# Threshold attention and a squared-ReLU layer: rounding instructions, thresholds and a bank order moved

## Chip, cores and metric

One core of a Trainium2 chip runs the whole program. The metric is the device time of one execution in microseconds (us), smaller is better. A core has five engines that run their own queues side by side: TensorE (PE, matrix products; PEld is its weight load), VectorE (DVE), ScalarE (ACT), GpSimd (POOL) and SyncE (SP, which issues most DMAs). SBUF is the on-chip memory, PSUM the eight banks that TensorE writes.

## What is computed

Batch 8, 8 heads, 576 positions, head width 64. For every head

```
scores = q @ k.T / 8
keep   = scores >= rowmax(scores) - tau
attn   = exp(where(keep, scores, -1e9) - rowmax);  attn /= rowsum + 1e-9
x      = attn @ v                       # heads side by side: 4608 x 512
out    = relu(x @ w_in)**2 @ w_out      # 512 -> 2048 -> 512
```

All data are float32; the two weight matrices come in as 64-bit words whose two halves the kernel combines ("rounding").

## The kernel before

**Attention** is worked in visits and steps. A visit is a pair of heads of one batch; a step is one block of 128 query rows of that visit. The first four visits have two steps each (steps 0 to 7), the next four have three (steps 8 to 19), the later ones four or five. In a step TensorE makes the scores in PSUM (`scores`, L280 or L273), VectorE takes two row maxima (`maxima`, L317), ScalarE takes the exponentials into `w`, VectorE masks them with the threshold and sums them (`threshold`, L354, then L356 for the sum and L357 for the reciprocal), and GpSimd divides (`divide`, L362 and L364). Two steps later TensorE transposes `w` (`turn`, L408), ScalarE copies that out (L409), and the values are mixed (`mix`, L524).

The threshold is `maximum - 8 tau`. In the early steps (`early_exponents`, steps 0 to 10) VectorE adds it for both columns (L329), with the constant `ntau8` that GpSimd scaled at the start (L1036); then ScalarE makes a bias (L332) and an exponential (L333) for each of the two halves of the step. In later steps (`exponents`) ScalarE makes bias (L339), threshold (L340) and exponentials (L342).

**Weights** come in 32 pieces into a ring of three areas and are rounded in stages (`round_weights`): stage 0 is two ScalarE instructions (L149, L150), stage 1 a shift and stage 2 a mask on VectorE (L152, L154), stage 3 a product on GpSimd (L156), and `end_rounding` adds and places the piece on GpSimd (L158) and loads the next. An early step does stage 0 for its own piece and the other stages for the piece of the step before, after `threshold` and `divide`. From step 11 on a step rounds one piece, but four steps (12, 15, 18 and 22) round two.

**The layer** is worked in chunks of 256 tokens: `mlp_in` (L571), a square (L581, L582), then for chunk 0 `mlp_out` (L753, copied out by L759) and for later chunks products of halves (L788). A planner, `fill`, puts as many of these pieces into each step as an estimated rate asks for; it knows costs written in the source, not measured times, so the order of work is fixed when the program is built.

**Banks.** Chunk 0 takes banks 6 and 7 of PSUM in turn (`take`), later work takes the bank that was used longest ago (`next_bank`, from the list `oldest`, which `last_used` reorders).

What an early step ends with, and the middle of a later one:

```
threshold(n, i)
divide(n, i)
while rounding:
    p = rounding.popleft()
    for stage in (1, 2, 3):
        round_weights(p, stage)
    end_rounding(p)
```

Each engine takes its instructions in the order in which the source issues them; waits on other engines are semaphores.

Of the kernel before, what the change touches and what calls it, by code (L numbers as in the profile page):

```python
# [9 lines left out]
FP32 = mybir.dt.float32  # L10
U32 = mybir.dt.uint32
AF = mybir.ActivationFunctionType
ALU = mybir.AluOpType
# [6 lines left out]
def kernel(  # L20
# [10 lines left out]
    nc = tc.nc  # L31
# [3 lines left out]
    P = 128  # L35
# [11 lines left out]
    SCALE = 0.125  # L47
# [4 lines left out]
    const = ctx.enter_context(tc.tile_pool(name="const", bufs=1))  # L52
# [2 lines left out]

    ident = const.tile([P, P], FP32, name="ident")
    seen = const.tile([P, 1], FP32, name="seen")
    ntau8 = const.tile([P, 2], FP32, name="ntau8")

    w_in_sb = const.tile([P, NMC, d_ff], FP32, name="w_in_sb")  # L60

# [19 lines left out]
    at = RAW * 2 * WP  # L81
# [24 lines left out]
    bank = [big[:, x * 512:(x + 1) * 512] for x in range(8)]  # L106
# [14 lines left out]
    def weight_piece(i):  # L121

        if i < n_in:
            f, c = BLK[i // NMC], i % NMC
            cols = slice(f * WP, (f + 1) * WP)
            return moe_w_in[c * P:(c + 1) * P, cols], w_in_sb[:, c, cols].rearrange("p (h d) -> p h d", h=2)
        i -= n_in
        to = wo[:, Q00:Q01 + 1:Q01 - Q00, i, :] if i < HF else wo[:, Q10:Q11 + 1, i - HF, :]
        return moe_w_out[i * P:(i + 1) * P, :], to

    def weight_area(i):
        at = (i % RAW) * 2 * WP
        return spare[:, at:at + 2 * WP]
# [4 lines left out]
    def round_weights(i, stage):  # L138

        words = weight_area(i).bitcast(U32).rearrange("p (n w) -> p n w", w=2)
        lo, hi = words[:, :, 0], words[:, :, 1]
        t, e, d = (turned[:, (i % 3 * 3 + x) * WP:(i % 3 * 3 + x + 1) * WP] for x in range(3))
        tu, eu = t.bitcast(U32), e.bitcast(U32)
        if stage == 0:
            nc.scalar.activation(out=e, in_=hi.bitcast(FP32), func=AF.Prelu, scale=2.0 ** -112, alpha=-2.0 ** 32)  # L149
            nc.scalar.activation(out=d, in_=lo, func=AF.Copy, scale=2.0 ** -52)  # L150
        elif stage == 1:
            nc.vector.tensor_scalar(out=tu, in0=eu, scalar1=3, scalar2=None, op0=ALU.logical_shift_left)  # L152
        elif stage == 2:
            nc.vector.tensor_scalar(out=eu, in0=tu, scalar1=0xFF800000, scalar2=None, op0=ALU.bitwise_and)  # L154
        elif stage == 3:
            nc.gpsimd.tensor_tensor(out=d, in0=d, in1=e, op=ALU.mult)  # L156
        else:
            nc.gpsimd.tensor_tensor(out=weight_piece(i)[1], in0=t.rearrange("p (h d) -> p h d", h=2),  # L158
                                    in1=d.rearrange("p (h d) -> p h d", h=2), op=ALU.add)
# [166 lines left out]
    def early_exponents(vis, i):  # L326

        w, sc, st = weights[vis, i]
        nc.vector.tensor_tensor(out=st[:, 1, 0:len(sc)], in0=st[:, 0, 0:len(sc)], in1=ntau8[:, 0:len(sc)], op=ALU.add)  # L329
        for u in range(len(sc)):  # L330
            bias = st[:, 2, u:u + 1]
            nc.scalar.activation(out=bias, in_=st[:, 0, u:u + 1], func=AF.Copy, scale=-SCALE)  # L332
            nc.scalar.activation(out=w[:, u, :].rearrange("p (h k) -> p h k", h=2), in_=sc[u],  # L333
                                 func=AF.Exp, bias=bias, scale=SCALE)

    def exponents(vis, i):
        w, sc, st = weights[vis, i]
        mx, thr, bias = (st[:, j, 0:len(sc)] for j in range(3))
        nc.scalar.activation(out=bias, in_=mx, func=AF.Copy, scale=-SCALE)  # L339
        nc.scalar.activation(out=thr, in_=mx, func=AF.Identity, bias=ntau8[:, 0:1])  # L340
        for u in range(len(sc)):
            nc.scalar.activation(out=w[:, u, :].rearrange("p (h k) -> p h k", h=2), in_=sc[u],  # L342
                                 func=AF.Exp, bias=bias[:, u:u + 1], scale=SCALE)

    def threshold(vis, i):

        w, sc, st = weights[vis, i]
        n = len(sc)  # L350
        thr, sm, den, rcp = (st[:, j, 0:n] for j in (1, 3, 5, 6))
        for u in range(n):
            wu = w[:, u, :].rearrange("p (h k) -> p h k", h=2)
            nc.vector.scalar_tensor_tensor(out=wu, in0=sc[u], scalar=thr[:, u:u + 1], in1=wu,  # L354
                                           op0=ALU.is_ge, op1=ALU.mult, accum_out=sm[:, u:u + 1])
        nc.vector.tensor_reduce(out=den, in_=st[:, 3:5, 0:n].rearrange("p j u -> p u j"), axis=AX.X, op=ALU.max)  # L356
        nc.vector.reciprocal(rcp, den)  # L357

# [8 lines left out]
    used = {"tx": 0, "mm": 0, "bank": 7}  # L367
# [2 lines left out]

    def take(what, among):
        used[what] += 1
        return bank[among[used[what] % len(among)]]

    def next_bank():

# [5 lines left out]
    def last_used(x):  # L382
        oldest.remove(x)
        oldest.append(x)
# [464 lines left out]
    def by_dma(n):  # L849

        return n >= 3 * HP - 1
# [113 lines left out]
    for s, (n, i) in enumerate(steps):  # L965
        if s < HP * FIRST:
            x = int(n > 0 and i == 1)
        else:
            x = 0 if s == early_to - 1 else 2 if (n, i) in ((HP + 1, FIRST + 1), (2 * HP - 2, FIRST + 1), (2 * HP - 1, FIRST + 1), (2 * HP, FIRST)) else 1
# [49 lines left out]

    load_qk(0)  # L1020
    make_identity(nc, ident)
    nc.gpsimd.dma_start(out=ntau8[:, 0:1], in_=tau.to_broadcast([P, 1]))
    nc.gpsimd.memset(qmid, 0.0)
    for t in vs:
        for u in range(2):
# [6 lines left out]
    load_v(0)  # L1032
    for i in range(RAW):
        load_weights(i)
    for x in (1, 0):
        nc.gpsimd.tensor_scalar(out=ntau8[:, x:x + 1], in0=ntau8[:, 0:1], scalar1=-1.0 / SCALE, scalar2=None, op0=ALU.mult)  # L1036
    keep_busy(20, 7)
    done = 0
    rounded_by = [0]
# [89 lines left out]
    def early_step(s):  # L1129


        n, i = steps[s]
        first, last = i == visits[n][1][0], i == visits[n][1][-1]
        now = list(range(sum(pieces[:s]), sum(pieces[:s + 1])))
        if first and n and n + 2 < 2 * HP:
            load_qk(n + 2)
        if s == 0:
            scores(0)()
            early_exponents(n, i)
            keep_busy(18, 7)  # L1140
            held_back.append(scores(1))
            prep_part(k, 1)
        elif s == 1:
            prep_part(q, 1)
            held_back.pop()()
            early_exponents(n, i)
            scores(2)()
            early_exponents(*steps[2])
        elif s > 2:
            scores(s)()  # L1150
            early_exponents(n, i)
        copies = [turn(*steps[s - 2], part) for part in range(3)] if s > 1 else []
        if s == 2:
            keep_busy(12, 4)
        if s > 1 and (first or n >= HP and i == FIRST + 1) and not (first and n >= HP):
            prep_part(k, n + 1)
        if s > 1 and last:
            prep_part(q, n + 1)
        for fn in copies:
            fn()  # L1160
        if s in mixes:
            mix(*mixes[s])
            for j in chunk_at.get(s, ()):
                add_chunk(j)
        if first:
            split_left(n)
        for p in now:
            round_weights(p, 0)
        threshold(n, i)
        divide(n, i)  # L1170
        while rounding:
            p = rounding.popleft()
            for stage in (1, 2, 3):
                round_weights(p, stage)
            end_rounding(p)
        rounding.extend(now)
        assert s < early_to - 1 or not now
        if first and n:
            load_v(n)

    rounding = deque()
    for s in range(END + 1):
# [13 lines left out]
        now = []  # L1196
        if on:
            n, i = steps[s]
            at = visits[n][1].index(i)
            last = at == len(visits[n][1]) - 1  # L1200
            now = list(range(done, done + pieces[s]))
# [18 lines left out]
        if on:  # L1220
            exponents(n, i)
            if s and by_dma(steps[s - 1][0]):
                turn_last(s)
            for p in now[1:]:
                round_weights(p, 0)
            if at == 1:
                split_left(n)
            if lay:
                prep(n + 1)
            elif now:  # L1230
                for p in now:
                    round_weights(p, 1)
        if s in mixes and not old:
            mix(*mixes[s])
            for j in chunk_at.get(s, ()):
# [15 lines left out]
        if on:  # L1251
            threshold(n, i)
            for fn in prep_at[s] + load_at[s]:
                fn()
            if lay and now:
                round_weights(now[0], 1)
            if now:
                round_weights(now[0], 2)
                round_weights(now[0], 3)
            for p in now[1:]:  # L1260
                assert not lay
                round_weights(p, 2)
                round_weights(p, 3)
            if not at_once:
                divide(n, i)
# [60 lines left out]
```

## Time and profile before

| what | value |
|---|---|
| median of 3 runs | 1328.32 us (1327.66 to 1328.34) |
| the profiled execution: its time, its span | 1329.19 us, 1327.4 us |
| TensorE busy | 1292.5 us, 97% of the span |
| VectorE busy | 936.9 us, 71% |
| GpSimd busy | 786.3 us, 59% |
| ScalarE busy | 582.4 us, 44% |
| L329, threshold adds | 11, 4.1 us |
| L152, L154, VectorE's part of the rounding | 32 each, 24.1 and 21.6 us |
| L156, L158, GpSimd's part | 32 each, 40.9 and 42.5 us |

A row of the profile's timeline gives the start in us, the duration in us, the engine, the line of the source, the operation, output and inputs with their shapes, and in brackets the idle time before it and what ended it. A row of the waits gives who waited for whom, the total, how often, and the longest. Busy times by stretch give, for a piece of the span, the busy us of each engine. A busy TensorE is not TensorE at its peak.

### The profile page before, as it was taken

Reading aid. Unit: us, or ns where it says so; the run is one execution under the profiler, and the core shown is the slowest. Engines: PE = TensorE matmul, PEld = TensorE weight load, DVE = VectorE, ACT = ScalarE, POOL = GpSimd, SP = SyncE. Lnnn points to the kernel's source line nnn. Section 1 sums busy time; section 2 is a strip of 40 time slices with the busy share of each in tenths; the row PEclk is TensorE's granted clock in tenths of the full one; section 3 lists DMA queues with packets and bytes.
Section 4 is the critical chain, followed back from the end, with each engine's and each line's share of the span. In section 5 each row is a group of like instructions: output and inputs, shape, how many; then the busy total and the mean of one; then the engine's idle time right before and its main releaser. Section 6 shows DMA issues by size and latency. Waiting matters only on the chain.

```text
span 1327.4 us, 24734 instructions
## 1 busy us (share of the span) xinstructions
PE 1292.5 (97%) x8862; PEld 1070.4 (81%) x8862; DVE 936.9 (71%) x2037; ACT 582.4 (44%) x1342; POOL 786.3 (59%) x917
## 2 busy tenths in 40 slices
PE   7899999999999999999999999999999999999998
PEld 5666556888887879697878888888887988889997
DVE  6978876887787878778776777868686877622131
ACT  4777774335352626253534353434343434331321
POOL 3789974874846564565665655646574737454351
PEclk9999999999999999999999999999999999999999
DMA  6764531757687869676766867767686766520000
GB/s 128 154 160 121 152 85 26 166 134 178 166 188 168 196 152 207 146 195 157 151 165 159 181 152 180 174 126 180 146 194 135 189 161 153 160 53 9 9 17 17
DMA packets 320907, 185.48 MB, mean 140 GB/s; under 512 B 282224, under 2 KB 282256, under 8 KB 314384
## 3 DMA queue, kind: packets, MB, share of 16 engines
q1 hardware_dynamic: 309120, 115.78, 46.1%
q0 software_dynamic: 10000, 67.92, 12.8%
q8 instruction: 70, 1.15, 0.4%
q14 instruction: 53, 0.43, 0.1%
q10 hardware_dynamic: 1664, 0.21, 0.1%
HBM read 108.04 MB, written 68.42 MB: 133 GB/s over the span
## 4 chain that ended last, share of the span: by engine, by line
PE 83%; DVE 6%; DMA 4%; ACT 2%; POOL 2%; issue 2%; SPq 1%; DVEq 0%; ACTq 0%; POOLq 0%
PE big L682 29%; PE big L788 28%; PE big L524 10%; PE big L296 8%; PE big L571 3%; PE big L280 2%; DVE st L317 2%; DMA wT<-aside 1%; PE big L753 1%; DMA aside<-turned 1%; DVE w L354 1%; PE big L408 1%; SPq L185 1%; ACT w L342 1%; POOL w_in_sb L158 0%
## 5 line engine op out<-in xcount | busy, mean ns | idle before, releaser
L354 DVE SCALAR_TENSOR_TENSOR w<-big,st,w 128x576 f32<-128x576 f32 x269 | 207.1, 805 | 88.1 <-ACT w L342 87.6
L317 DVE TENSOR_REDUCE st<-big 128x1 f32<-128x576 f32 x288 | 204.3, 748 | 88.8 <-PE big L296 60.7
L364 POOL TENSOR_SCALAR w<-w,st 128x576 f32<-128x576 f32 x269 | 244.9, 919 | 27.8 <-DVE st L357 22.3
L788 PE MATMUL big<-wo,gsum 128*128 128x256 f32 x1088 | 243.8, 382 | 0.0
L788 PEld LDWEIGHTS big<-wo,gsum 128*128 128x128 f32 x1088 | 204.4, 190 | 37.0 <-issue 7.6
L682 PE MATMUL big<-xT,w_in_sb 128*128 128x128 f32 x1536 | 187.4, 277 | 1.3 <-DVE g L694 1.2
L682 PEld LDWEIGHTS big<-xT,w_in_sb 128*128 128x128 f32 x1536 | 178.5, 192 | 10.5 <-issue 7.7
L788 PE MATMUL big<-wo,g 128*128 128x256 f32 x816 | 185.3, 382 | 0.1
L342 ACT ACTIVATE w<-big,st 128x576 f32<-128x576 f32 x255 | 174.2, 734 | 0.2 <-POOL t L659 0.2
L788 PEld LDWEIGHTS big<-wo,g 128*128 128x128 f32 x816 | 151.6, 190 | 26.1 <-issue 6.5
L524 PE MATMUL big<-wT,vs 128*64 128x256 f32 (+5 forms) x1420 | 159.6, 389 | 5.8 <-DMA wT<-aside 3.7
L524 PEld LDWEIGHTS big<-wT,vs 128*64 128x64 f32 (+1 forms) x1420 | 85.6, 136 | 71.7 <-issue 20.7
L362 POOL TENSOR_SCALAR st<-st 128x2 f32<-128x2 f32 (+1 forms) x148 | 35.6, 241 | 181.2 <-DVE w L354 169.8
L339 ACT ACTIVATE st<-st 128x2 f32<-128x2 f32 (+1 forms) x137 | 27.9, 204 | 250.1 <-DVE st L317 248.8
L430 POOL DMA_DIRECT2D aside<-turned x50 | 29.9, 597 | 177.9 <-DVE turned L459 171.8
L694 DVE TENSOR_TENSOR g<-big,g 128x512 f32<-128x512 f32 x96 | 64.7, 677 | 83.4 <-PE big L682 77.8
L296 PE MATMUL big<-kT,qT 64*128 64x256 f32 (+3 forms) x768 | 106.9, 416 | 0.0
L296 PEld LDWEIGHTS big<-kT,qT 64*128 64x128 f32 x768 | 84.5, 186 | 14.5 <-issue 5.0
L690 ACT ACTIVATE g<-g 128x512 f32<-128x512 f32 x96 | 60.3, 628 | 63.7 <-DVE g L694 63.6
L561 POOL TENSOR_TENSOR gsum<-g 128x512 f32<-128x512 f32 x34 | 46.1, 1356 | 69.8 <-ACT g L691 60.2
L691 ACT ACTIVATE g<-g 128x512 f32<-128x512 f32 x128 | 80.7, 630 | 4.1
L453 DVE STREAM_TRANSPOSE turned<-w 128x512 f32<-128x512 f32 x100 | 70.3, 703 | 0.3 <-issue 0.3
(118 smaller groups left out, 2063.4 us busy)
## 6 DMA issues: line engine op xcount, KB each, us to landing
aside<-turned POOLq DMA_DIRECT2D x50, 1152.0 KB, 4.8
wT<-aside SPq DMA_DIRECT2D x200, 288.0 KB, 5.4
vs<-in_v_dram SPq DMA_DIRECT2D x72, 128.0 KB, 5.9
wo<-in_moe_w_in_dram SPq DMA_DIRECT2D x16, 512.0 KB, 4.4
wo<-in_moe_w_out_dram SPq DMA_DIRECT2D x16, 512.0 KB, 3.6
out_dram<-osb POOLq DMA_DIRECT2D x32, 256.0 KB, 4.1
kl<-in_k_dram SPq DMA_DIRECT2D x113, 72.0 KB, 3.4
ql<-in_q_dram SPq DMA_DIRECT2D x112, 72.0 KB, 5.8
```

The lines of the kernel that those rows point to most:

```text
L296: nc.tensor.matmul(big[to, at + x0:at + x1], lhsT, keys[u * D:(u + 1) * D, x0:x1], start=True, stop=True)
L317: nc.vector.tensor_reduce(out=mx[:, u:u + 1], in_=sc[u], axis=AX.XY, op=ALU.max)
L342: nc.scalar.activation(out=w[:, u, :].rearrange("p (h k) -> p h k", h=2), in_=sc[u], func=AF.Exp, bias=bias[:, u:u + 1], scale=SCALE)
L354: nc.vector.scalar_tensor_tensor(out=wu, in0=sc[u], scalar=thr[:, u:u + 1], in1=wu, op0=ALU.is_ge, op1=ALU.mult, accum_out=sm[:, u:u + 1])
L364: nc.gpsimd.tensor_scalar(out=w[:, u, :], in0=w[:, u, :], scalar1=z[:, u:u + 1], scalar2=rcp[:, u:u + 1], op0=ALU.add, op1=ALU.mult)
L453: move(wb[:, 0:h, :, :], whole_[:, 0, :, :, :])
L524: nc.tensor.matmul(ps[u * D:(u + 1) * D, :], vs[n % 2][rows, u * (NBLK + 1) + c, :], wT[rows, at // REST:(at + ps.shape[1]) // REST, NBLK ...
L682: nc.tensor.matmul(to[:, f, :], factor(j, p, q, c)[:, f * P:(f + 1) * P], part[:, c, :], start=(p in "125" and f == 0 and c == 0), stop=(p ...
L690: nc.scalar.activation(out=to, in_=to if src is None else src, func=AF.Relu)
L691: nc.scalar.activation(out=to, in_=to, func=AF.Square)
L694: nc.vector.tensor_tensor(out=x, in0=to, in1=x, op=ALU.add)
L788: nc.tensor.matmul(to, left[:, f, :], wo[:, slot, f, :], start=(f == 0), stop=(f == HF - 1))
```

## The change

Four edits.

- VectorE's threshold add of the early steps becomes an identity with a bias on ScalarE, issued after the first exponential. `ntau8` has one column, scaled once.
- In early steps stages 1 and 2 of the waiting piece are issued after the masks and before the sum and the reciprocal (`between`). Stage 3 and the end stay behind the divide.
- In steps with two pieces stage 1 of the second piece is issued behind the masks, after stage 3 of the first piece, where it was ahead of the masks.
- A bank that chunk 0 takes counts as used (`last_used`), so that chunk 1 begins with the one used longest ago.

```diff
 def early_exponents(vis, i):
     w, sc, st = weights[vis, i]
-    nc.vector.tensor_tensor(out=st[:, 1, 0:len(sc)], in0=st[:, 0, 0:len(sc)], in1=ntau8[:, 0:len(sc)], op=ALU.add)
     for u in range(len(sc)):
         bias = st[:, 2, u:u + 1]
         nc.scalar.activation(out=bias, in_=st[:, 0, u:u + 1], func=AF.Copy, scale=-SCALE)
         nc.scalar.activation(out=w[:, u, :].rearrange(...), in_=sc[u], func=AF.Exp, bias=bias, scale=SCALE)
+        if u == 0:
+            nc.scalar.activation(out=st[:, 1, 0:len(sc)], in_=st[:, 0, 0:len(sc)], func=AF.Identity, bias=ntau8)
...
-def threshold(vis, i):
+def threshold(vis, i, between=()):
...
             nc.vector.scalar_tensor_tensor(out=wu, in0=sc[u], scalar=thr[:, u:u + 1], in1=wu, ...)
+    for fn in between:
+        fn()
     nc.vector.tensor_reduce(out=den, ...)
     nc.vector.reciprocal(rcp, den)
...
 def take(what, among):
     used[what] += 1
-    return bank[among[used[what] % len(among)]]
+    at = among[used[what] % len(among)]
+    if what == "mm":
+        last_used(at)
+    return bank[at]
...
-for x in (1, 0):
-    nc.gpsimd.tensor_scalar(out=ntau8[:, x:x + 1], in0=ntau8[:, 0:1], ...)
+nc.gpsimd.tensor_scalar(out=ntau8, in0=ntau8, ...)
...
 # early_step
-threshold(n, i)
+threshold(n, i, [lambda p=p, x=x: round_weights(p, x) for p in rounding for x in (1, 2)])
 divide(n, i)
 while rounding:
     p = rounding.popleft()
-    for stage in (1, 2, 3):
-        round_weights(p, stage)
+    round_weights(p, 3)
     end_rounding(p)
...
 # later steps, ahead of the masks
-for p in now:
-    round_weights(p, 1)
+round_weights(now[0], 1)
...
 # behind the masks
 for p in now[1:]:
+    round_weights(p, 1)
     round_weights(p, 2)
     round_weights(p, 3)
```

More of the change, by code (lines that the diff above doesn't have):

```diff
@@ L57 @@
     seen = const.tile([P, 1], FP32, name="seen")
-    ntau8 = const.tile([P, 2], FP32, name="ntau8")
+    ntau8 = const.tile([P, 1], FP32, name="ntau8")
     w_in_sb = const.tile([P, NMC, d_ff], FP32, name="w_in_sb")
@@ L339, in exponents @@
         nc.scalar.activation(out=bias, in_=mx, func=AF.Copy, scale=-SCALE)
-        nc.scalar.activation(out=thr, in_=mx, func=AF.Identity, bias=ntau8[:, 0:1])
+        nc.scalar.activation(out=thr, in_=mx, func=AF.Identity, bias=ntau8)
         for u in range(len(sc)):
@@ L1021 @@
     make_identity(nc, ident)
-    nc.gpsimd.dma_start(out=ntau8[:, 0:1], in_=tau.to_broadcast([P, 1]))
+    nc.gpsimd.dma_start(out=ntau8, in_=tau.to_broadcast([P, 1]))
     nc.gpsimd.memset(qmid, 0.0)
@@ L1034 @@
         load_weights(i)
-    for x in (1, 0):
-        nc.gpsimd.tensor_scalar(out=ntau8[:, x:x + 1], in0=ntau8[:, 0:1], scalar1=-1.0 / SCALE, scalar2=None, op0=ALU.mult)
+    nc.gpsimd.tensor_scalar(out=ntau8, in0=ntau8, scalar1=-1.0 / SCALE, scalar2=None, op0=ALU.mult)
     keep_busy(20, 7)
```

## The prediction

> **What bounds the kernel now.** I read the page's busy times first, then busy times by stretch, the waits of the stretches that the change touches, and the engines' timelines there. Names: "step n" is one round of scores, and M is when its first row maximum (L317) starts, M4 = 28.03 us, M5 = 33.73, and so on. "First/second mask" are the two L354, "first/second exponential" the two L333 or L342.
>
> The page, part 1:
> ```profile
> PE 1292.5 (97%) x8862; PEld 1070.4 (81%) x8862; DVE 936.9 (71%) x2037; ACT 582.4 (44%) x1342; POOL 786.3 (59%) x917
> ```
> TensorE bounds the whole, but the edits lie where it does not. Busy times by stretch (PE, PEld, DVE, ACT, POOL, granted clock, DMA share):
> ```profile
> 9.40:64.05 54.65, 43.43 (x356) 33.42 (x357) 49.50 (x117) 37.62 (x91) 30.41 (x40) 0.96 0.70 153
> 64.05:146.00 81.95, 76.72 (x443) 53.05 (x443) 67.42 (x136) 61.52 (x143) 73.54 (x76) 0.98 0.52 140
> 210.00:220.00 10.00, 8.94 (x51) 7.29 (x50) 3.36 (x9) 2.52 (x8) 3.69 (x5) 1.00 0.15 54
> ```
> Up to 64 us VectorE is the busiest (49.5 of 54.65) and TensorE has 11 us of gaps. From 64 to 146 us GpSimd (73.5 of 82) and TensorE (76.7) share the bound. After that TensorE has work without gaps, except once near 211 us. What is gained before 220 us therefore moves the rest earlier as a block; nothing later waits for a clock time.
>
> VectorE's timeline in step 4 and at 60 us, then GpSimd's at the same times:
> ```profile
> 32.43 0.41 DVE L152 TENSOR_SCALAR turned<-turned 128x512 uint32<-128x512 uint32 x1
> 32.87 0.94 DVE L154 TENSOR_SCALAR turned<-turned 128x512 uint32<-128x512 uint32 x1
> 33.73 1.40 DVE L317 TENSOR_REDUCE st<-big 128x1 f32<-128x576 f32 x2
> 35.17 0.59 DVE L329 TENSOR_TENSOR st<-st,ntau 128x2 f32<-128x2 f32 x1
> ...
> 60.03 1.24 DVE L329 TENSOR_TENSOR st<-st,ntau 128x1 f32<-128x1 f32 x1
> ```
> ```profile
> 32.71 1.79 POOL L364 TENSOR_SCALAR wo<-wo,st 128x576 f32<-128x576 f32 x2 [0.28 <-PE big L280]
> ...
> 59.99 1.26 POOL L156 TENSOR_TENSOR turned<-turned 128x512 f32<-128x512 f32 x1
> ```
> L154 takes 0.41 us alone and 0.94 while GpSimd divides; a threshold add of two columns takes 0.16 alone and 0.59 or 1.24 beside GpSimd.
>
> Waits from 64 to 146 us (us, times, longest), then TensorE's timeline:
> ```profile
> POOL turned L156 <- DVE turned L154: 6.1, 5, 2.6
> DVE turned L152 <- ACT turned L149: 5.7, 4, 2.0
> ```
> ```profile
> 62.45 1.57 PE L280 MATMUL big<-kT,qT 64*128 64x288 f32 x8 [2.03 <-DVE wo L354]
> ...
> 211.59 5.45 PE L571 MATMUL big<-xT,w_in_sb 128*128 128x256 f32 x24 [1.06 <-ACT osb L759]
> ```
> The four waits of L152 are the second roundings of steps 12, 15, 18 and 22, each with that step's masks behind it on VectorE. At 211.59 chunk 1's first matmul waits for the last copy out of chunk 0's bank.
>
> [...] the trace has one ACT_TABLE_LOAD (1.28 us, at 2.82) for all exponentials, copies and identities, so the moved add brings no load. [...] Here the gap of 2.03 us is followed by a granted clock of 0.50 from 64.0 to 66.3 us.
>
> **The early adds (11, L329) and the roundings ahead of the sum (steps 4, 6, 8, 9, 10).** VectorE loses 11 adds: 4.1 us busy. ScalarE gains 11 identities between the exponentials; L340 starts 0.10 after L339 and L342 0.19 after L340, so I take 0.12 us for each on what follows. The first mask now waits for the threshold, the second for a later exponential. Working a pair, from M5:
>
> Step 5 (no rounding): bias +0.79, exponential +1.07 (as now), threshold +1.71 (0.64 after an exponential), ready +2.03; second bias +1.83, exponential +2.10, its mask 0.77 later (50.27 to 51.04), +2.87. Now the masks start at +2.31 and +3.02. The next scores give M6 2.11 after the first mask (36.04 to 38.15): +4.14 against +4.42. ScalarE is free 3.03 after its second exponential, +5.13, so step 6's bias is held to that (it wanted 4.93): here **ScalarE takes VectorE's place** and some of the gain. Step 6: exponential 5.41, threshold 6.05, second exponential 6.44, second mask 7.21; L152 at 8.01, L154 +0.44 without GpSimd (whose divide now starts after them), sum +0.48, reciprocal +0.19, M7 at 9.30. Now it is 43.79 - 33.73 = 10.06: **-0.76**.
>
> The same sums for steps 3 and 4 give 9.30 against 9.82 (**-0.52**) and for 7 and 8 9.30 against 9.69 (**-0.39**; step 8 has no transposes, so the late exponential counts in full). Steps 0 to 2 lose the add without filling ScalarE: 10.93 to 11.23 and some hundredths, **-0.35**. Step 9 would gain 0.78, but GpSimd's L156 and L158, now behind a later divide (M9 + 1.75 to 4.37), lie across L152: **-0.3**. In step 10 the first mask starts 0.33 earlier, so TensorE's scores do too: **-0.34**; VectorE's L154 may be locked out by L158, which puts VectorE +0.28 there, not TensorE. Sum: -0.52 - 0.76 - 0.39 - 0.35 - 0.3 - 0.34 = **-2.7 us** at step 12. GpSimd's later divide is covered: the transposes that read it come two steps later (32.71 to 38.78). Bounds: -1.3 (0.19 per identity, more locking) to -3.6 (no locking in 9 and 10). The gap of 2.03 shrinks to 1.7; the half-rate matmuls behind it cost about 1.5 us (nine L408 in 2.37, elsewhere 1.20, and 0.33 in L280). Whether they keep their rate I can't tell: I take a quarter, **-0.4**, bounds +0.5 and -1.5.
>
> **The second roundings (steps 12, 15, 18, 22).** L152 of the second piece leaves the place ahead of the masks. In step 12 the masks start at 73.8 in place of 75.32, GpSimd (idle 2.59 before 77.67) starts L156 about 1.1 us earlier; TensorE, nearly full there, takes 0.2 to 0.6. In step 15:
> ```profile
> 90.52 1.23 DVE L152 TENSOR_SCALAR turned<-turned 128x512 uint32<-128x512 uint32 x1
> 92.95 0.87 DVE L152 TENSOR_SCALAR turned<-turned 128x512 uint32<-128x512 uint32 x1 [1.21 <-ACT turned L149]
> 93.74 0.80 DVE L354 SCALAR_TENSOR_TENSOR w<-big,st,w 128x576 f32<-128x576 f32 x1
> ...
> 95.60 0.97 DVE L154 TENSOR_SCALAR turned<-turned 128x512 uint32<-128x512 uint32 x2
> ```
> The masks come 1.9 us earlier, but L154, L152, L154 then stand in a row, each between two GpSimd operations: L158 to 94.8, L582 to 96.1, L156 to 97.55. GpSimd's second L156 starts near 98.0 against 97.6 (**+0.4**), and the next step's maximum at 97.95 against 96.49. Behind that maximum are two transposes, a mask and the scores of step 17; of its 1.46 us, 1.0 is slack (mask over at 99.14, L280 at 100.12), so again about +0.5. Steps 18 and 22 have the same spacing. The sites together: -1.0 and 3 x 0.4 = **+0.2**; bounds -2 and +4.
>
> **Banks.** Chunk 0's matmuls now age their bank, so chunk 1 starts on bank 7, whose copy began at 209.01 and took 0.59, in place of bank 6, copied until 211.5. TensorE's wait of 1.06 goes; bank 6 is wanted 8 matmuls (1.9 us) later, after its copy. **-1.06**, bounds -1.1 and -0.5. The order of instructions agrees: the wait on ScalarE moves to the ninth matmul, TensorE and SP are otherwise in the same order, so no DMA is moved. One GpSimd scale of tau (0.28) goes at 6.4 us, where it is hidden. Nothing else of VectorE, L741 or the DMAs changes.
>
> Sum: -2.7 - 0.4 + 0.2 - 1.06 = -3.96. The profiled execution took 1329.19 (span 1327.4), so about 1325.2; its 0.87 above the median of 1328.32 goes off too: **1324.4 us**.
>
> **Rivals.** (1) ScalarE becomes the bound from the start: each identity costs 0.19 to 0.3 on the second mask, the early part gives -0.8 (the early adds' isolated 0.16 less), the sites +0.2, the bank -1.06: 1326.7. For it: ScalarE is held in three of the pairs. Against: steps 4, 6, 9 lose 0.5 of locking for certain. (2) Slower: at steps 15, 18, 22 VectorE's L154 of the second piece stands behind a whole GpSimd L156, and the next maximum, late by 1.5, sets scores, masks and divides. It decides once the lateness passes the 1.0 of slack and GpSimd can't make it up: 3 x 1.5 = 4.5, early part -1.3, bank -1.06: 1330.5. For it: GpSimd is 95% busy there. Against: ScalarE's L150, which waits for L158 (102.62), lets VectorE catch up. (3) The orders bring only the bank: 1327.3.
>
> **Chances.** Mine (1320.5 to 1325.6) 0.62; (1) and (3), within 0.2% of 1328.32 (2.7 us, about what a measurement of this kernel can tell from no change), 0.20; (2) 0.18. The range takes in (1), (3) and the near half of (2): 1320.5 to 1330.0.
>
> **What would show it.** Right: no L329; L154 at 0.43 before 64 us; M7 - M5 near 9.3; L571 after 209 us without its wait. Wrong: masks of steps 4 to 9 waiting for ScalarE by more than 0.2; maxima after steps 15, 18, 22 late and TensorE waiting over 1 us for masks behind them.

## The result and the profile after

The changed kernel takes **1323.07 us** (median of 6 runs, 1322.66 to 1323.33) against 1328.3 us of the kernel before in the same session (1327.66 to 1328.9): 0.9961 of it, 95% interval 0.9949 to 0.9973. Run again on another chip it took 1322.77 against 1328.95: 0.9957 (0.9944 to 0.9971). It is faster, by 5.2 to 6.2 us; 1324.4 was predicted. The profiled execution of the changed kernel took 1322.66 us with a span of 1320.9; the one of before took 1329.19 with 1327.4.

In the changed file the lines after L328 have moved: the identity is L335, the early bias and exponential L331 and L332, the masks L355, sum and reciprocal L359 and L360, GpSimd's divide L365 and L367, the transposes of the weights L414, `mlp_in` L577. L152 to L158 (the rounding), L280 (scores) and L317 (maxima) have kept theirs. M is again the start of a step's first L317.

The page, part 1. VectorE has 11 instructions fewer and still 4.9 us more busy time, ScalarE has the 11 more:
```profile
PE 1291.0 (98%) x8862; PEld 1069.3 (81%) x8862; DVE 941.8 (71%) x2026; ACT 583.8 (44%) x1353; POOL 785.8 (59%) x916
```
Busy times by stretch (PE, PEld, DVE, ACT, POOL, granted clock, DMA share), cut at the same events as before: M0 to M11, then up to step 24, then ten microseconds around chunk 1's first matmul:
```profile
8.64:60.41 51.77, 44.51 (x361) 34.13 (x361) 45.52 (x106) 39.50 (x103) 29.22 (x39) 0.97 0.70 157
60.41:140.50 80.09, 75.13 (x437) 51.87 (x437) 76.62 (x137) 60.99 (x143) 74.26 (x76) 1.00 0.56 147
205.00:215.00 10.00, 10.00 (x63) 7.87 (x64) 4.75 (x10) 4.25 (x11) 3.69 (x5) 1.00 0.15 54
```
M0 to M11 is 2.9 us shorter. VectorE has 4.0 us less to do there. In the second row it has 9 us more, though nothing was added: those are the roundings that now lie beside GpSimd, longer (L152 and L154 take 55.2 us in all, 45.7 in before) and off the path. In the third row TensorE is never idle.

VectorE's timeline around steps 4, 5 and 10:
```profile
31.01 0.43 DVE L154 TENSOR_SCALAR turned<-turned 128x512 uint32<-128x512 uint32 x1
...
33.70 0.82 DVE L355 SCALAR_TENSOR_TENSOR w<-big,st,w 128x576 f32<-128x576 f32 x1 [0.33 <-ACT st L331]
...
58.21 0.59 DVE L152 TENSOR_SCALAR turned<-turned 128x512 uint32<-128x512 uint32 x1
58.84 1.39 DVE L154 TENSOR_SCALAR turned<-turned 128x512 uint32<-128x512 uint32 x1
```
L154 is back to 0.43 us in step 4, now ahead of GpSimd's divide; beside it, in before, it took 0.94. What the prediction and e11's expectation call locking or a lock is this longer time; its cause the traces don't show. The mask of step 5 starts 2.08 behind M5 (31.62) and waits for ScalarE, as predicted (2.03), by 0.33. In step 10 the other side shows: both operations lie beside GpSimd's products of the piece before, and together take 2.0 us in place of 0.86.

TensorE's timeline at step 11's scores, at step 17's, and at chunk 1's first matmul:
```profile
58.35 1.24 PE L280 MATMUL big<-kT,qT 64*128 64x288 f32 x8 [1.73 <-DVE wo L355]
...
94.58 1.24 PE L280 MATMUL big<-kT,qT 64*128 64x288 f32 x8 [0.48 <-DVE wo L355]
...
204.94 5.34 PE L577 MATMUL big<-xT,w_in_sb 128*128 128x256 f32 x24
```
The gap ahead of step 11 is 1.73 in place of 2.03, and the scores behind it run at full rate (1.24 against 1.57). L577 has no wait left.

VectorE and then GpSimd at step 15, where the three roundings stand in a row:
```profile
87.85 1.51 DVE L154 TENSOR_SCALAR turned<-turned 128x512 uint32<-128x512 uint32 x1
89.28 1.26 DVE L152 TENSOR_SCALAR turned<-turned 128x512 uint32<-128x512 uint32 x1
90.57 1.38 DVE L154 TENSOR_SCALAR turned<-turned 128x512 uint32<-128x512 uint32 x1
91.87 0.74 DVE L317 TENSOR_REDUCE st<-big 128x1 f32<-128x576 f32 x1
```
```profile
87.79 1.28 POOL L158 TENSOR_TENSOR w_in_sb<-turned 128x512 f32<-128x512 f32 x1
89.02 1.23 POOL L588 TENSOR_TENSOR g<-g 128x512 f32<-128x512 f32 x1
90.21 1.45 POOL L156 TENSOR_TENSOR turned<-turned 128x512 f32<-128x512 f32 x1
92.09 1.28 POOL L156 TENSOR_TENSOR turned<-turned 128x512 f32<-128x512 f32 x1 [0.43 <-DVE turned L154]
```
Each of the three ends 0.29 us behind the end of one of GpSimd's operations (L158 at 89.07, L588 at 90.25, L156 at 91.66), and M16 comes 8.40 behind M15 in place of 7.31. GpSimd's wait for L154 from step 11 to step 24 has all the same fallen (us, times, longest; it was 6.1, 5, 2.6):
```profile
POOL turned L156 <- DVE turned L154: 2.4, 4, 1.2
```

### The profile page after: what moved, and what is told of

Read it like the earlier page. It is cut to its first block, busy times and chain, and to the rows that moved or that the text cites. A ratio compares the mean times of both kernels' runs of the same rounds, so it can differ in the third digit from the quotient of the medians.

```text
span 1320.9 us, 24730 instructions
## 1 busy us (share of the span) xinstructions
PE 1291.0 (98%) x8862; PEld 1069.3 (81%) x8862; DVE 941.8 (71%) x2026; ACT 583.8 (44%) x1353; POOL 785.8 (59%) x916
## 4 chain that ended last, share of the span: by engine, by line
PE 84%; DVE 5%; DMA 3%; ACT 2%; POOL 1%; issue 1%; SPq 0%; DVEq 0%; POOLq 0%
PE big L688 29%; PE big L794 28%; PE big L530 10%; PE big L296 8%; PE big L577 4%; PE big L280 2%; PE big L759 2%; DMA wT<-aside 1%; DMA aside<-turned 1%; PE big L414 1%; DVE w L355 1%; DVE st L317 1%; ACT w L343 1%; DVE turned L154 0%; POOL w_in_sb L158 0%
## 5 line engine op out<-in xcount | busy, mean ns | idle before, releaser
L355 DVE SCALAR_TENSOR_TENSOR w<-big,st,w 128x576 f32<-128x576 f32 x269 | 207.8, 807 | 87.2 <-ACT w L343 85.3
L317 DVE TENSOR_REDUCE st<-big 128x1 f32<-128x576 f32 x288 | 204.2, 748 | 83.4 <-PE big L296 61.4
L367 POOL TENSOR_SCALAR w<-w,st 128x576 f32<-128x576 f32 x269 | 243.8, 915 | 29.4 <-DVE st L360 24.7
L530 PE MATMUL big<-wT,vs 128*64 128x320 f32 (+5 forms) x1420 | 159.7, 389 | 6.7 <-DMA wT<-aside 3.3
L365 POOL TENSOR_SCALAR st<-st 128x2 f32<-128x2 f32 (+1 forms) x148 | 35.8, 242 | 176.6 <-DVE w L355 166.0
```

The costliest lines, as they stand in the source:

```text
L317: nc.vector.tensor_reduce(out=mx[:, u:u + 1], in_=sc[u], axis=AX.XY, op=ALU.max)
L367: nc.gpsimd.tensor_scalar(out=w[:, u, :], in0=w[:, u, :], scalar1=z[:, u:u + 1], scalar2=rcp[:, u:u + 1], op0=ALU.add, op1=ALU.mult)
L530: nc.tensor.matmul(ps[u * D:(u + 1) * D, :], vs[n % 2][rows, u * (NBLK + 1) + c, :], wT[rows, at // REST:(at + ps.shape[1]) // REST, NBLK ...
```

## The experiments

Two theories stood at the start. **A**: the time went where the sum had it, into the early chain of masks and roundings and into the bank, with the four sites of the second rounding near zero. **B**: much of it is TensorE's clock, whose half-rate stretch behind step 11's wait (granted clock 0.50 in before, 1.00 in the changed kernel) comes and goes. Each kernel's time is set against the kernel before on its own chip.

### One part at a time (e1 to e4)

Each is the kernel before with one part of the diff of the section on the change: the identity on ScalarE (e1); `between` ahead of the sum (e2); the second piece's stage 1 behind the masks (e3); `last_used` in `take` (e4).

**e1.** 

> Only the threshold adds of the early steps move from VectorE to ScalarE. Theory 1 (the prediction's sums: VectorE's chain sets the early steps, ScalarE takes part of the gain): steps 0 to 3 -0.7, steps 3/4 0, 5/6 -0.3, 7/8 +0.1, 9 and 10 -0.7, together -1.5 us against before; and if the gap of TensorE ahead of step 11 falls from 2.03 to about 1.7 and its clock then stays at full rate (window 56 to 62 us), -1.3 more, -2.8. Theory 2 (ScalarE becomes the bound at once): -0.5 to +0.5. Theory 3 (what the change brought beyond the sums is not the clock): -1.5 with a half-rate stretch still there.

Measured: 1327.04 us, 0.9984 (0.9978 to 0.9991). Steps 3/4, 5/6 and 7/8 take 9.83, 9.81 and 9.79 (9.82, 10.06 and 9.69 before), steps 9 and 10 together 9.60 in place of 10.57. Steps 0 to 2 (M0 to M3) take 13.89 in place of 14.51. So the adds' move alone shortens the start, pair 5/6 and steps 9 and 10; in the other pairs L154 still takes 0.94 beside the divide and eats the gain. From M0 to M13 the trace is 1.36 us shorter, with a half-rate stretch (62.1 to 65.5 us) still there: that is theory 3 of the expectation. The median fell by 2.2, more than the trace explains.

**e2.** 

> Only the roundings of the early steps go ahead of the sum and the reciprocal. Theory 1 ([...] the divide that comes later is covered): L154 falls to 0.43 in steps 4, 6 and 8, 0.34 us each, -1.0; in step 9 it meets L158 and in step 10 L156, 0 to +0.3; together -0.9 us, and the gap ahead of step 11 stays at 2.0, so the half-rate stretch stays. Theory 2 (the later divide holds up TensorE's transposes): +0.5 or more, with TensorE waiting for GpSimd in steps 6 to 10. Theory 3 (no effect alone[...]): -0.2.

Measured: 1325.23 us, 0.9972 (0.9961 to 0.9983): 4.0 us less, where 0.9 was expected. VectorE's timeline in step 4 of this kernel (L358 is the sum, and L329 still the add):
```profile
32.49 0.43 DVE L154 TENSOR_SCALAR turned<-turned 128x512 uint32<-128x512 uint32 x1
32.83 0.15 DVE L358 TENSOR_REDUCE st<-st 128x2 f32<-128x4 f32 x1
...
34.54 0.47 DVE L329 TENSOR_TENSOR st<-st,ntau 128x2 f32<-128x2 f32 x1
```
L154 has lost its 0.51 and the step 0.62: the sum follows L154's start by 0.34 where L152 to L154 took 0.46. The three pairs gain 0.62, 0.40 and 0.50 (0.34 each was expected) and step 9 gains 0.34, where none was. By M11 the kernel is 1.65 ahead of before; behind it comes no half-rate stretch (the wait is 1.31 us), which the expectation had as staying, and from step 13 on it is 3.1 ahead.

**e3.** 

> Only VectorE's part of the second rounding goes behind the masks (steps 12, 15, 18, 22). Theory 1 (the masks come earlier, but three operations of VectorE in a row each wait for a GpSimd operation, and the next maximum is late by as much): -0.5 to +0.5 us; L152 or L154 of the second piece at about 1.3, maxima of steps 16, 19, 23 about 1 us later against those of steps 15, 18, 22, TensorE no later at step 25. Theory 2 (the wait of VectorE for ScalarE's L149, 5.7 us before, was on the path): -2 to -4. Theory 3 (the late maxima set the steps): +2 to +4.

Measured: 1327.83 us, 0.9990 (0.9983 to 0.9997): 1.4 us less, more than theory 1 allowed (0.5). Up to step 11 its instructions are those of before, one by one. TensorE at step 11 in this kernel, then the same stretch of time in before and in e3:
```profile
63.45 1.24 PE L280 MATMUL big<-kT,qT 64*128 64x288 f32 x8 [2.04 <-DVE wo L354]
```
```profile
64.00:66.50 2.50, 2.50 (x12) 2.13 (x11) 1.76 (x3) 1.45 (x5) 2.42 (x3) 0.50 0.60 98
```
```profile
64.00:66.50 2.50, 2.26 (x17) 1.58 (x14) 2.31 (x5) 1.69 (x6) 2.39 (x3) 1.00 0.49 75
```
The wait is as long as before (2.04 and 2.03 us) and the clock behind it full instead of half. In turn, this execution ran at half rate from 14 to 24 us, before only from about 19 to 22. So the same wait is sometimes followed by half rate and sometimes not, and theory B has something to stand on. The maxima of steps 16, 19 and 23 came 0.5, 1.1 and 1.1 us late against those of steps 15, 18 and 22, and the lateness was made up, as in the whole change. From M3 to M25 the trace is 2.0 us shorter than that of before, and 1.4 of these lie between M10 and M13, where before ran at half rate and e3 did not.

**e4.** 

> Only the banks of chunk 0 count as used. Theory 1 (TensorE's wait for the copy out of bank 6 goes and nothing else moves): -1.0 to -1.2 us, the first matmul of chunk 1 without a wait, all times before 209 us as before. Theory 2 (the wait was covered by a later one, the first aside transfer at 400 us or the copies that follow): 0.

Measured: 1327.32 us, 0.9987 (0.9981 to 0.9994). TensorE's timeline at chunk 1's first matmul (L574 here):
```profile
210.67 0.49 PE L411 MATMUL big<-ident,w 128*128 128x128 f32 x3
211.00 1.25 PE L574 MATMUL big<-xT,w_in_sb 128*128 128x256 f32 x5
```
It starts 0.33 behind the transposes in front of it, in place of 1.55: 1.22 us at the place itself, and M36 is 1.33 earlier against M35. Theory 1 (-1.0 to -1.2) holds in kind, with -1.33 at the place; the median fell by 1.9.

The four medians fell by 2.2, 4.0, 1.4 and 1.9 us, together 9.5, and the whole change gave 5.2 to 6.2. But all four are set against one median of before, 1329.22; in a later session on the same chip (that of e9) before took 1328.23, and with that number the four falls sum to 5.5. An error of this one number counts four times. The traces are steadier: from M3 to M36 the four kernels are 0.8, 3.1, 2.0 and 1.2 us shorter than before, together 7.1, and the whole change 5.3. Of the excess, some 0.7 us is the half-rate stretch, which e2 and e3 both escape, so that it is counted twice, and 0.86 lies in steps 9 and 10, where the first two parts don't add up (shown with e7).

### The whole but for one part (e5 to e8)

e5 is the changed kernel once more; e6, e7 and e8 leave out the first, second and third of these parts.

**e5.** 

> The whole change once more, beside three kernels that each leave one part of it out. Both theories: 0.9961 of before, 5 us less, as first measured; the next maxima of the early steps 9.16 to 9.20 apart per pair, the one of step 10 late (5.02 behind step 9's, the second operation of the rounding 1.39 beside GpSimd).

Measured: 1322.77 us, 0.9957; its steps agree with those of the first profile to some hundredths.

**e6.** 

> All but the adds' move to ScalarE (VectorE keeps them). If the parts add up, this loses the 2.1 us that the move alone gave: 0.9977 of before. If the move's gain in steps 9 and 10 is swallowed by the rounding ahead of the reciprocal (with both, steps 9 and 10 took 10.45 together, against 10.57 before and 9.60 with the move alone), and if a part of its gain was the clock, it loses only what the pairs show: about 0.5 for the start and 0.3 for pair 5/6, some 0.7 to 1.3 us, 0.9966 to 0.9971.

Measured: 1324.20 us (1322.23 to 1324.44), 0.9963 (0.9950 to 0.9975): 1.4 us more than e5. At M36 its profiled execution is 1.6 behind e5's, of which 0.66 lay already ahead of M0, before any instruction of the change; so the part is worth about 0.9 by the trace, 0.66 of it between M0 and M3. That is the second case of the expectation (0.7 to 1.3); the medians' 1.4 lies between its two cases, and their intervals don't part these. Alone the medians had given it 2.2.

**e7.** 

> All but the roundings ahead of the reciprocal. If the parts add up, this loses 3.7 us: 0.9989 of before. If half of the 3.7 was the clock (1.4 to 2.0 us of it came in one stretch at 64 to 66 us that ran at half rate before), and the move of the adds gives steps 9 and 10 back (9.60 for both, against 10.45), it loses 0.6 x 3 pairs less 0.85, about 1.0, and 1.3 more only if the half-rate stretch comes back: 0.9969, or 0.9979 with the stretch. The gap of TensorE ahead of the scores of step 11 is then about 1.9 us.

Measured: 1324.65 us, 0.9969 (0.9957 to 0.9980): 1.9 us more than e5, by the traces 1.75, of which 0.66 ahead of M0. It loses 0.64 in each of the three pairs and wins 0.86 back in steps 9 and 10: 1.1 us, as worked out, without the half-rate stretch. The wait ahead of step 11 is 1.90 us, the same as in e1. The stretch behind it in e1, then in e7:
```profile
62.00:65.00 3.00, 3.00 (x13) 2.40 (x12) 2.46 (x4) 2.52 (x7) 2.90 (x3) 0.51 0.56 82
```
```profile
62.00:65.00 3.00, 2.76 (x19) 2.06 (x16) 2.41 (x5) 2.60 (x8) 2.90 (x3) 1.00 0.63 92
```
Equal waits, half the clock in one and the full clock in the other.

The traces say what tells these two apart. In the profiles of before and after the changes of the granted clock lie whole multiples of 3.413 us apart: before runs at 0.50 from 18.86 to 22.27 us and from 63.23 to 66.65, with 40.96 us (12 x 3.413) between the two, after from 17.23 to 20.65; the half-rate stretches noted here for other profiles last about 3.4 or 10 us. This raster fell differently on the program from execution to execution. Cut along it, e1 and then e7, ahead of and behind the scores of step 11:
```profile
58.65:62.06 3.41, 1.54 (x11) 1.06 (x12) 2.23 (x8) 3.33 (x8) 3.14 (x4) 1.00 0.80 219
62.06:65.48 3.42, 3.42 (x13) 2.73 (x12) 2.88 (x6) 3.00 (x8) 2.84 (x3) 0.50 0.54 81
```
```profile
56.54:59.95 3.41, 2.72 (x32) 2.15 (x30) 2.72 (x8) 2.56 (x7) 2.99 (x4) 1.00 0.51 155
59.95:63.36 3.41, 2.05 (x14) 1.32 (x14) 2.82 (x8) 3.12 (x10) 3.14 (x5) 1.00 0.95 202
```
In e1 nearly the whole wait falls into one stretch of the raster, which leaves TensorE 1.54 us busy in it; in e7 it is cut in two (2.72 and 2.05 busy). Before and e3 differ in the same way: 1.38 busy (59.82 to 63.23 us), then half rate, in before; 3.05 and 1.74, then the full clock, in e3. Around step 11 half rate came behind stretches with at most 1.54 us busy (before, e1, e4) and not behind 1.68 (e8), 1.74 (e3, e5) or 1.84 (the changed kernel, 54.78 to 58.19 us). Busy time alone does not part the cases elsewhere: at the start 1.69 was followed by half rate in e3, and in e9 2.33 (35.4 to 38.8 us).

**e8.** 

> All but the second roundings' move behind the masks. If the parts add up, this loses the 1.3 us that it gave alone: 0.9971 of before. If it is as good as nothing within the whole (the four sites summed to -0.1 us between step 12 and step 25 in the whole change's trace), no change beyond 0.3 us: 0.9959 to 0.9963, the maxima of steps 16, 19 and 23 about 1 us earlier against those ahead of them and the end of that stage unmoved.

Measured: 1323.74 us, 0.9961 (0.9949 to 0.9974): 1.0 us more than e5, more than the 0.3 expected of "as good as nothing", though the ratio lies inside the range named for it. The traces decide: at step 12 it is 1.37 behind e5 (all of that there by step 3, ahead of the part left out), at step 25 1.86. The third part is worth about 0.5 us within the whole, not zero.

### The clock taken out (e9, e10, e12) and a version past the change (e11)

TensorE is given something to do in its waits, with a helper that the kernel has already:

```diff
 # early_step, s == 1
     early_exponents(n, i)
+    keep_busy(16, 0)
     scores(2)()
...
 # early_step, behind the mix
+if s == 10:
+    keep_busy(8, (4, 5, 6, 7)[(used["tx"] + 1) % 4])
```

e9 is before with both, e12 before with the second alone, e10 the changed kernel with both (4 in place of 8).

**e9.** 

> The kernel before, with transposes of the identity that nobody reads put into two waits of TensorE: 16 ahead of the scores of step 2 (of some 3.7 us without work between 12.1 and 17.1 us about half stays empty, since the banks are all taken) and 8 ahead of those of step 11 (a wait of 2.03 us of which about 0.9 us stays, until a bank is copied out). If the half-rate stretch at 63 to 66 us in the profile of before follows the wait, it is gone, and it cost about 1.3 us in the executions that had it: 0.9990 to 0.9997 of before. If the stretch has nothing to do with the wait, it is still there in about two of three executions and the time is that of before (0.9998 to 1.0005).

**e10.** 

> The whole change with the same transposes (16, and 4 since the wait ahead of step 11's scores is 1.73 us there). Against e9 the clock has less to say, so the distance of the two is what the change gives by its instructions: early steps 2.7, banks 1.2, sites 0.1, together about 4.0 us. If the clock gave the change nothing, the distance is the 5.2 to 6.2 us of the two runs without transposes. Expected 1322.0 us at the chip's 1329.0 of before.

Measured: e9 1325.81 us (1324.08 to 1327.16), 0.9979 (0.9972 to 0.9987), below the whole range expected of it; e10 1321.86 us, 0.9946 (0.9933 to 0.9958). The distance is **3.95 us** where 4.0 was expected, against 5.2 to 6.2 without the transposes; e9's executions spread over 3.1 us, so the closeness is in part luck. TensorE at step 11 in e9, then in e10 (L324 are the transposes):
```profile
61.18 1.09 PE L324 MATMUL big<-ident 128*128 128x128 f32 x8 [1.05 <-ACT wT L409]
```
```profile
59.12 0.66 PE L324 MATMUL big<-ident 128*128 128x128 f32 x4 [1.17 <-ACT wT L415]
```
The waits are cut to 1.05 and 1.17 us, and both kernels run at the full clock (1.00) behind them. From M10 to M13 e9 gains 0.72 us on before. The half rate at about 18 to 22 us stays in both; TensorE still waits 2.52 and 2.33 us just ahead of it. And e9 has a half-rate stretch that before does not have, from 38.8 to 42.2 us (it costs 0.25 in pair 5/6 and is made up in pair 7/8). So the filling changed the clock, but did not even it out everywhere.

**e12.** 

> The kernel before with the 8 transposes ahead of step 11's scores alone; it parts the 2.4 us that e9 gave with both fillings. If the half-rate stretch behind step 11's wait was what they saved, this gives most of it: the maximum of step 13 some 0.7 us earlier against the start, and 0.9982 to 0.9990 of before. If the 16 at the start did it (the half rate between 14 and 23 us), this gives little: 0.9993 to 1.0000.

Measured: 1327.34 us, 0.9990 (0.9983 to 0.9997). From M10 to M13 it gains the same 0.71, with the clock at 1.00 from 61 to 67 us. That is the upper end of the first case: by the ratios the half rate behind step 11 is about half of what e9 gained. The start is not the other half, as far as the profile shows: from M0 to M3 e9 takes 14.47 us and before 14.51. In the profiles of all four filled kernels (e9 to e12) the stretch from M40 to M100 (253 to 745 us in before) takes 490.8 to 491.1 us, in the ten others 491.6 to 492.3, at the full clock (1.00 in before and in the changed kernel) and without any edit there; why is open. The profiled execution of e12 had a bad start (half rate from 14 to 24 us, granted clock 0.51 from 14 to 23, 1.6 us lost between M1 and M3), which shows how far a single profile can stand from a median.

So both theories hold a part, A by far the larger. From M0 to M36 the profile of the changed kernel is 5.99 us shorter than that of before, and e10's 4.79 shorter than e9's. Of the 1.2 between, 0.6 lie from M10 to M13: that is the clock at step 11, B's part (0.7 by e9 and e12). The other 0.6 lie ahead of M3 and are not clock: e6 and e7 have the same M0 (9.47) and the same half-rate stretch (19.0 to 22.4 us), differ up to step 3 by the adds' move alone, and need 14.53 and 13.91 us from M0 to M3. In e10 the 16 transposes take this gain away, as step 2's maximum then waits 0.43 us for its scores. The instructions therefore give about 5.3 of the 6.0 us. The medians' distances are known to about 1.5 us only.

**e11** is e10 with the rounding of step 9 left to step 10, ahead of that step's mask:

```diff
+if s == 10:
+    p = rounding.popleft()
+    for stage in (1, 2, 3):
+        round_weights(p, stage)
+    end_rounding(p)
-threshold(n, i, [... for p in rounding for x in (1, 2)])
+threshold(n, i, [... for p in rounding if s != 9 for x in (1, 2)])
 divide(n, i)
-while rounding:
+while rounding and s != 9:
...
-    rounded_by.append(state["rounded"])
+    rounded_by.append(state["rounded"] + (s == 10))
```

> As e10, and the rounding that step 9 does between its masks and its sum goes to step 10, ahead of that step's mask, where VectorE waits 0.92 us for ScalarE. If VectorE sets the maximum of step 10, that comes up to 0.9 us earlier (4.5 instead of 5.4 behind step 9's), and the two operations take 0.43 each, or 0.43 and 0.94 beside GpSimd's division, so that the maximum of step 11 comes 0.4 to 0.9 us earlier: 0.4 to 0.9 us below e10. If they meet GpSimd's lock ahead of the mask (0.9 and 1.4 instead of 0.43), the mask is late by what was won, and the time is e10's.

Measured: 1321.11 us, 0.9940 (0.9926 to 0.9953): 0.75 below e10, by overlapping intervals. VectorE in step 10:
```profile
56.62 0.47 DVE L152 TENSOR_SCALAR turned<-turned 128x512 uint32<-128x512 uint32 x1
57.12 0.93 DVE L154 TENSOR_SCALAR turned<-turned 128x512 uint32<-128x512 uint32 x1
57.98 0.80 DVE L355 SCALAR_TENSOR_TENSOR wo<-big,st,wo 128x576 f32<-128x576 f32 x1
58.71 1.06 DVE L152 TENSOR_SCALAR turned<-turned 128x512 uint32<-128x512 uint32 x1
59.80 1.37 DVE L154 TENSOR_SCALAR turned<-turned 128x512 uint32<-128x512 uint32 x1
```
M10 is 4.43 behind M9 in place of 5.42, the 0.9 us hoped for. The rounding filled the wait ahead of the mask and ran over it (L154 at 0.93 beside the divide): the mask starts 2.46 behind M10 in place of 2.08. And the next two operations still took longer, beside GpSimd's work (1.06 and 1.37 in place of 0.43). By step 13 about 0.23 of the 0.99 is left. The best version of the study, but its distance to e10 is not settled by these runs: the trace shows 0.23 where the medians have 0.75.

## Why the prediction was right, and where it was not

The sign and the chain of causes hold, and the time lies 1.3 us under the forecast. The stated range (1320.5 to 1330.0) took in no change at all, so the time alone proves little and the terms have to be looked at. Their sum was -3.96; from M0 to M36 the profiles give -5.99. Every term came out on the faster side. Step by step, with e9 against e10 where the clock at step 11 would mix in:

- **Early part, -2.7.** Right in kind and too small: about -3.2. Up to M12 e10 gains 2.78 on e9 (0.28 behind at M0, 2.50 ahead at M12), but that this is close to 2.7 is luck, since the filling hides the start. Steps 0 to 2 gave -0.62 (e7 against e6; predicted -0.35), the three pairs -2.03 (predicted -1.67). In the changed kernel pairs 3/4, 5/6 and 7/8 take 9.20, 9.18 and 9.16, where 9.30 was worked out for each. The identity costs 0.18 to 0.19 us of ScalarE and not 0.12 (L335 at 10.31, the next bias at 10.50), which alone would have made them longer; the term that was off the other way is the tail on VectorE: the sum starts 0.34 behind L154's start and not 0.48, and the next maximum 0.08 behind the reciprocal and not 0.18. Step 9 gave -0.35 (predicted -0.3); step 10 +0.23 on VectorE (predicted +0.28), and on TensorE -0.23 (predicted -0.34).
- **The parts lean on each other.** e1 and e2 were each to give a piece of this sum. With both, steps 9 and 10 take 10.45; with the adds' move alone, 9.60. The rounding ahead of the sum takes back in these two steps what the adds' move gave, since GpSimd's L156 and L158, later by the divide, lie across it (L152 takes 0.88 us in step 9 of e10, L154 1.39 in its step 10). The prediction had this for steps 9 and 10, and e7 shows it as 0.86 us.
- **Clock, -0.4.** It was an estimate of a quarter of 1.5 us. Filling the wait of step 11 moves the trace by 1.2 at M12 and, as some of it is made up, by 0.71 (e12) and 0.72 (e9) at M13. So the half rate cost 0.7 and not 1.5, and the changed kernel had none of it in both its profiled executions (1.00 from 58.19 to 65.02 us in the first): the whole term and not a quarter. The changed kernel's profile is also 0.76 ahead at M0. That is not the change (M0 lies between 8.64 and 9.76 us in the 14 profiles, in no order of the kernels), so the pair of profiles, 6.5 us apart, flatters the change, and the prediction's 0.87 for the profiled execution's distance to its median points the same way. That half rate follows a wait of this length was the author's reading of one profile; e3 (2.04 us) and e7 (1.90 us) ran at 1.00 behind theirs. Whether a wait of 1.9 to 2.0 us cost the clock went with how it fell on the raster, which a single profile doesn't tell of other executions.
- **Second roundings, +0.2.** The step that failed by most: it was -1.0 at step 12 and 3 x 0.4 at the others. From e9 to e10 step 12 gives -0.97 (M12 to M15), and the three others +0.22 in all (M15 to M24): -0.75 and not +0.2. The maxima are late as predicted in kind, by 1.1 (predicted 1.46), but that is hardly above the 1.0 of slack which the prediction itself had counted; TensorE waits 0.48 and 0.62 us for the mask in steps 17 and 20, and by the next step with two pieces the lateness is gone. Rival 2 (slower, from a lateness past the slack) falls by the same number.
- **Bank, -1.06.** At the place itself -1.22, between M35 and M36 -1.33. The prediction took the wait that the profile prints (1.06); the time from the last transpose to the first matmul was longer than this wait and went with it.
- **Rival 1** had the right price, 0.19 for each identity, and the masks do wait for ScalarE by 0.33; it was not the bound, as VectorE's tail overlaps more. A wait of over 0.2 there had been named as a sign of error, and that sign was badly chosen: the prediction's own working had the mask at 2.03, with VectorE free by then. **Rival 3** (the bank alone) falls with e1 and e2.

VectorE and TensorE at step 16 show how a late maximum is paid for. VectorE's timeline in e9, then in e10:
```profile
94.60 0.96 DVE L154 TENSOR_SCALAR turned<-turned 128x512 uint32<-128x512 uint32 x2
95.49 0.75 DVE L317 TENSOR_REDUCE st<-big 128x1 f32<-128x576 f32 x1
```
```profile
91.80 1.38 DVE L154 TENSOR_SCALAR turned<-turned 128x512 uint32<-128x512 uint32 x1
93.09 0.74 DVE L317 TENSOR_REDUCE st<-big 128x1 f32<-128x576 f32 x1
```
In e9 the two L154 stand together behind the masks and take 0.96; in e10 the last of the three operations takes 1.38 by itself, as in the changed kernel at step 15. M16 is 2.40 ahead of e9's after M15 was 3.47 ahead, and M18 is 3.40 ahead again.

What stays open: e10's lead on e9 is 4.51 us at M36 in the traces and 3.95 by the medians (e9's profiled execution, 1326.51, is 0.7 above its median), so the parts are sure to a few tenths each and their sum not better than that. What sets the clock is open, too: TensorE's busy time in the stretch of 3.413 us ahead parts the two cases around step 11 (1.54 against 1.68), and not at the start. How often the changed kernel meets the half rate behind its 1.73 us was not counted.

## What to carry to other kernels

Put a VectorE operation that takes longer beside GpSimd where GpSimd has nothing to do yet (here L154: 0.43 us in place of 0.94): ahead of the small result that GpSimd's next operation waits for. Where that can't be had, move it off the path and compare its lateness with the slack behind it, as the slack decides and not the longer busy time. Don't price single parts of a change by medians that differ by less than the reference itself wanders: four parts measured alone summed to 9.5 us against one median of before and to 5.5 against another, and the whole gave 5.2 to 6.2. Price them stage by stage in traces, between the same events. Filler work can take a half-rate stretch out of such a comparison (0.7 us here), but it can also cover a gain, as it did with 0.6 us at the start.

## What the runs showed of the hardware

- **Roundings on VectorE took longer beside GpSimd.** L154 took 0.43 us in step 4 of the changed kernel and 0.94 beside the divide in before. At step 15 of the changed kernel VectorE's three roundings took 1.51, 1.26 and 1.38 us in place of 0.42 or 0.43 each, and each ended 0.29 us behind the end of one of GpSimd's operations (89.07, 90.25 and 91.66), which follow each other directly: here work in a row on both sides went one for one.
- **The clock changed on a raster.** Its changes lie whole multiples of 3.413 us apart in the profiles of before and after, and around step 11 half rate came behind stretches in which TensorE was busy for 1.38 to 1.54 us, not behind 1.68 and more (figures with e7).
- **A wait for a DMA varied from execution to execution.** TensorE's wait for blocks that pass through HBM (`aside`), three in each kernel, in the profiles of before, after and e10 (us, times, longest):
```profile
PE big L524 <- DMA wT<-aside: 3.7, 3, 1.3
```
```profile
PE big L530 <- DMA wT<-aside: 3.3, 3, 1.4
```
```profile
PE big L530 <- DMA wT<-aside: 2.0, 3, 0.7
```
Over all the profiles it lies between 1.9 and 3.7 us, with the changed kernel itself at 3.3 and 3.0. No edit touches it; a difference of 1 us between two profiles that arises there says nothing of the edit.
